# Sliding-window attention and a low-rank mixer on one core: load order, the order of chunk 0's second matmuls, one-slot values for two batches, and two copies of transposed Q/K

## The chip, the cores and the metric

The kernel runs on one core of one Trainium2 chip. A core has a matrix engine (TensorE, PE in the profile; PEld is its weight load), a vector engine (VectorE, DVE), a scalar engine (ScalarE, ACT), GpSimd (POOL), a queue engine (SyncE, SP) and 16 DMA engines. Each engine runs its own instructions in program order and waits for the others on semaphores. DMAs are issued here from POOL (loads that cast from float32 to bfloat16) and from SP (stores and transposes). The metric is the device time of one execution in microseconds (us), less is better.

## The reference

There are 8 batches of 576 tokens, 8 heads of 64 dimensions. Each query sees its own key and the 63 before it. The attention's output goes, laid out as (batch, token, 512), through a low-rank mixing over tokens and an MLP, both with a residual.

```python
mask = (rel >= 0) & (rel < 64)                      # rel = query position - key position
attn = softmax(where(mask, q @ k.T / 8, -1e9))
x = (attn @ v)                                      # as (batch, 576, 512)
u = x + ((x.transpose(0, 2, 1) @ U) @ V).transpose(0, 2, 1)   # U: 576x32, V: 32x576
out = u + maximum(u @ w_ch1, 0) @ w_ch2             # 512x2048, 2048x512
```

## The kernel before

**Chunks and slots.** The 4608 tokens of all batches are cut into 9 chunks of 512. For each chunk c the MLP is a list of 32 steps of four matmuls: 16 first matmuls `ch1(i)` (a `psA` tile, then a relu `c1_i` on DVE or ACT, as the lists `DVE_RELU` say) and 16 second ones `ch2(t, quarter)`, four token tiles t in four quarters of the inner dimension. After the last quarter DVE adds `u` into `osb`, and SP stores it. Each step is followed by a slot, a list of pieces of the next batch's attention (b = c + 1). The tables `PLACE`, `PLACE_1` (chunk 0, batch 1) and `PLACE_2` (chunk 1, batch 2) give each piece its slot. The program's order on every engine is written out by these tables; nothing is rescheduled. Slot 31 is the last one of a chunk that has a step ahead of it.

**Attention of one batch.** Q and K must stand transposed in `qf` and `kf`. For batches 0 and 1 the loads are grouped (`kg`, `qg`) and PE transposes them (pieces T). From batch 2 on they are loaded in five token tiles into `kn`, `qn`, and SP transposes them by DMA (pieces TX, ten a batch). There is one `kf` and one `qf` for all batches. Pieces S are the scores of head pairs with their exponent on ACT; SC8 is the same for the last 64 queries, the only one that reads token tile 4. M multiplies by the mask on DVE. PV multiplies by the values: for batches 0 to 2 one piece for each token tile (`PV(t)`), from batch 3 on all of them in one (`PVA`), which needs two `ps_big` buffers, one `ps_tp` and one `mm` buffer (`xe`). DVE divides by the sums and writes `xs`. U and V are the low-rank products (`pshh`, `psv`; DVE then adds into `un`). UT transposes `un` into `uTc`, which the next chunk's first matmuls read: on PE through the single `ps_tp` buffer with a copy on ACT for batches 1 and 2, and by SP's DMA from batch 3 on.

**Values.** The values stand in `vA`; `vB` holds the same rows moved by 64, copied from `vA` (`shift_v`): by POOL for batches 0 and 1, by DVE in slot 8 or 24 for the later ones.

**PSUM.** After the start the pool `mm` has three buffers, used in turn by `psA`, `psU`, `xe` and SC8's `high`. `ps_big` has two, `ps_tp` one.

**POOL's queue.** In this order: K and Q of batch 0, V of batch 0, w1 in halves, seven V copies, K and Q of batch 1, V of batch 1, w2 in four quarters, seven V copies, then for batches 2 to 7 K/Q and V. A DMA waits until the eighth before it has landed.

**SP's queue.** In program order: the stores of chunk c and the transposes of the slots. In chunk 0 the first store stands ahead of batch 2's transposes, which begin in slot 20; the others stand among and behind them.

Of the kernel before, what the change touches and what calls it, by code (L numbers as in the profile page):

```python
# [8 lines left out]
ACT = mybir.ActivationFunctionType  # L9
# [7 lines left out]
def kernel(  # L17
# [11 lines left out]
    nc = tc.nc  # L29
# [13 lines left out]
    NXB = 2  # L43
    NXU = 3
    GP = S // GR
# [13 lines left out]
    const = ctx.enter_context(tc.tile_pool(name="const", bufs=1))  # L59
    kg_pool = ctx.enter_context(tc.tile_pool(name="kg", bufs=4))  # L60
    uT_pool = ctx.enter_context(tc.tile_pool(name="uT", bufs=3))
# [28 lines left out]
    vB = [const.tile([P, NFULL, H, VW], BF16, name=f"vB{i}") for i in range(2)]  # L90
    kn = [const.tile([P, NT, H, D], BF16, name=f"kn{i}") for i in range(2)]
    qn = [const.tile([P, NT, H, D], BF16, name=f"qn{i}") for i in range(2)]

    kf = const.tile([P, NT * HP * P], BF16, name="kf")
    qf = const.tile([P, NT * HP * P], BF16, name="qf")
    kt, qt = ([f[:, j * S : (j + 1) * S] for j in range(HP)] for f in (kf, qf))
    kx, qx = (f.rearrange("p (t j w) -> p t j w", t=NT, j=HP) for f in (kf, qf))
    pts = const.tile([P, HP, 2, NB - 1, W], BF16, name="pts")
# [5 lines left out]
    def load_kq(b, split):  # L104
        grouped = b < NGR
        if grouped:
            kb = kg_pool.tile([GP, H, GR, D], BF16, name="kg")
            qb = kg_pool.tile([GP, H, GR, D], BF16, name="qg")
        else:
            kb, qb = kn[b % 2], qn[b % 2]  # L110
        loaded[b] = (kb, qb)
        if grouped:
            step = 4 if split else H
            for h0 in range(0, H, step):
                hs = slice(h0, h0 + step)
                for t, src in ((kb, k), (qb, q)):
                    nc.gpsimd.dma_start(  # L117
                        out=t[:, hs, :, :].rearrange("p h c d -> p h (c d)"),
                        in_=src[b, hs, :, :].rearrange("h (p c) d -> p h (c d)", c=GR),
                    )  # L120
                    yield
        else:
            for t in range(NT):
                rows = P if t < NFULL else W
                for dst, src in ((kb, k), (qb, q)):
                    nc.gpsimd.dma_start(  # L126
                        out=dst[0:rows, t, :, :],
                        in_=src[b, :, t * P : t * P + rows, :].rearrange("h p d -> p h d"),
                    )
                yield  # L130
# [15 lines left out]
    def shift_v(b, copy, tiles):  # L146
        va, vb = vA[b % 2], vB[b % 2]
        lo, hi = tiles.start, tiles.stop
        copy(out=vb[W:P, lo:hi, :, :], in_=va[W:P, lo:hi, :, :])
        last = min(hi, NFULL - 1)  # L150
        if lo < last:
            copy(out=vb[0:W, lo:last, :, :], in_=va[0:W, lo + 1 : last + 1, :, :])


# [38 lines left out]
    for i in range(2):  # L193
        nc.vector.memset(kn[i][W:P, NFULL, :, :], 0.0)
        nc.vector.memset(qn[i][W:P, NFULL, :, :], 0.0)

# [19 lines left out]
    for lo, hi in ((0, 1024), (1024, 2048)):  # L216
        nc.gpsimd.dma_start(out=w1b[:, :, lo:hi], in_=w1v[:, :, lo:hi])
    for t in range(NFULL):
        shift_v(0, nc.gpsimd.tensor_copy, range(t, t + 1))
    for _ in load_kq(1, False):  # L220
        pass
    load_v(1)
    w2v = moe_w_ch2.rearrange("(i p) m -> p i m", p=P)
    for i in range(0, NFC, 4):
        nc.gpsimd.dma_start(out=w2b[:, i : i + 4, :], in_=w2v[:, i : i + 4, :])
    for t in range(NFULL):
        shift_v(1, nc.gpsimd.tensor_copy, range(t, t + 1))

# [9 lines left out]
    def attention(b, spare=False):  # L238
# [5 lines left out]
        g0 = (b * S) // P  # L244
        pcs = {}

        grouped = b < NGR
# [28 lines left out]
        def TQ(j):  # L276
            def f():
                copy = nc.scalar.copy if spare and j == 3 else nc.vector.tensor_copy
                copy(out=place_of(qt, j), in_=tr(qb, j, b == 1))
            return f  # L280
# [80 lines left out]
        def SC8():  # L361
            if b >= NXU:

# [225 lines left out]
        def UT(t):  # L589
            def f():  # L590
                g = g0 + t
                dst = uT_of(g // TPC)[:, g % TPC, :, :]
                if b >= NXU:
                    nc.sync.dma_start_transpose(out=dst, in_=u_tiles[g][:])  # L594
                    return
# [13 lines left out]
        pcs["B"] = [SB(j) for j in range(HP + 1)]  # L609
        pcs["S"].insert(0 if b >= NXU else HP, SC8)  # L610
        if not spare:
            pcs["M"] = [MK(j) for j in range(HP)]
            pcs["M"].insert(0 if b >= NXU else HP, MK8)
        pcs["PV"] = [PVA] if b >= NXU else [PV(t) for t in range(NT)]
        pcs["U"] = [UM((t,)) for t in range(NT)] if spare else [UM(tuple(range(NT)))]
# [15 lines left out]

    DVE_RELU = {0: (8, 10, 11, 13, 15), 1: (2, 4, 6, 9, 10, 12, 13)}
    DVE_RELU_N = (0, 1, 2, 4, 5, 6, 8)

    def mlp(c):
        uTc = uT_of(c)
        c1 = [None] * NFC

        def ch1(i):
            def f():  # L640
                ps = psum["mm"].tile([P, CH], FP32, name="psA", tag="mm")
                for dc in range(NDC):
                    nc.tensor.matmul(  # L643
                        ps[:],
                        w1b[:, dc, i * P : (i + 1) * P],
                        uTc[:, :, dc, :],
                        start=(dc == 0),
                        stop=(dc == NDC - 1),
                    )
                c1[i] = c1_pool.tile([P, CH], BF16, name=f"c1_{i}")  # L650
                if i in DVE_RELU.get(c, DVE_RELU_N):
                    nc.vector.tensor_relu(out=c1[i][:], in_=ps[:])  # L652
                else:
                    nc.scalar.activation(out=c1[i][:], in_=ps[:], func=ACT.Relu)  # L654
            return f
# [23 lines left out]

        return [ch1(i) for i in range(NFC)] + [ch2(t, r) for t in range(TPC) for r in range(4)]  # L680

# [4 lines left out]
        "PV": [8],  # L686
        "TX": [6, 7, 8, 9, 10],
        "U": [14],
# [4 lines left out]
    PLACE_1 = {  # L693
        "T": [11, 11, 12, 12, 13, 13, 14, 14],
        "S": [12, 13, 14, 15, 15],
        "M": [13, 14, 15, 16, 16],
        "PV": [17, 17, 18, 19, 20],
        "U": [22],
        "V": [23, 24, 25],
        "UT": [25, 26, 27, 28, 29],  # L700
        "TX": [20, 22, 24, 26, 28],
    }
    PLACE_2 = {
        "S": [8, 8, 11, 11, 13],
        "M": [9, 10, 12, 13, 14],
        "PV": [16, 16, 18, 18, 20],
        "TX": [13, 14, 15, 16, 17],
        "U": [21],
        "V": [23, 24, 25],
        "UT": [25, 26, 27, 28, 29],  # L710
    }
# [4 lines left out]
    def turn_over(n, cols=CH):  # L716
# [16 lines left out]
    )  # L733
    pair = maskA[:, 0, 1:3, :].rearrange("p (o n) w -> p o (n w)", o=1)
    nc.vector.tensor_copy(
        out=maskA[:, 0, 3:7, :].rearrange("p (o n) w -> p o (n w)", o=2),
        in_=pair.to_broadcast([P, 2, 2 * W]),
    )
    nc.vector.tensor_copy(out=maskA[:, 0, 7, :], in_=maskA[:, 0, 1, :])
    nc.vector.tensor_scalar(  # L740
        out=maskB[:],
        in0=maskA[:, 0, :, :],
        scalar1=30000.0,
        scalar2=-30000.0,
        op0=ALU.mult,
        op1=ALU.add,
    )
    order = "K0 K1 B0 B1 Q0 Q1 S0 S1 K2 K3 B2 Q2 B3 Q3 S2 S3 B4 S4"
    for what in order.split():
        j = int(what[1])  # L750
        if what[0] in "SB":
            a[what[0]][j]()
        else:
            a["T"][2 * j + (what[0] == "Q")]()
        if what == "Q1":
            load_low_rank()
        turn_over({"B1": 1, "Q1": 1, "S1": 1, "Q3": 1}.get(what, 0))
    nc.vector.tensor_copy(out=maskA[:, 1, :, :], in_=maskA[:, 0, :, :])
    nc.scalar.copy(out=ub[0][:], in_=uf[0][:])
    nc.scalar.copy(out=vrep[:, W : W + S], in_=vf[:])  # L760
    for t in range(NT + 2):
# [7 lines left out]
    for f in [a["U"][NT - 1]] + a["X3"] + a["HT"]:  # L769
        f()  # L770
    first.close()
    psum["mm"] = ctx.enter_context(
        tc.tile_pool(name="ps_mm", bufs=3, space=bass.MemoryType.PSUM)
    )


    for c in range(NCH):
        slots = [[] for _ in range(NSLOT + 1)]

        def place(b, parts, where):  # L780
            if b not in att:
                att[b] = attention(b)
            for part in parts:
                for f, s in zip(att[b][part], where[part]):
                    slots[s].append(f)

        b = c + 1
        if b < B:
# [5 lines left out]
            if b + 2 < B:  # L794
                for _ in load_kq(b + 2, False):
                    pass
            where = {1: PLACE_1, 2: PLACE_2}.get(b, PLACE)
# [5 lines left out]
            for bs, slot in ((b, 8), (b + 1, 24)):  # L803
                if 1 < bs < B and (slot == 24) == (bs > 2):
                    slots[slot].append(
                        lambda bs=bs: shift_v(bs, nc.vector.tensor_copy, range(NFULL))
                    )
            place(b, ("S", "M", "PV"), where)
            if NXB <= b + 1 < B:
# [36 lines left out]
```

The softmax here doesn't subtract the row's maximum and nothing guards it: scores larger than these inputs give would overflow.

## Time and profile before

| | us |
|---|---|
| median of 7 runs | 321.74 (320.65 to 322.82) |
| the profiled execution | 320.83 |
| its span, first to last instruction | 319.1 |
| start to the first `psA` matmul | 23.41 |
| PE busy | 305.1 (96%) |
| DVE, ACT, POOL busy | 163.0, 101.8, 103.9 |

The span is shorter than the execution's time by 1.7 us, which lie outside of what the profile's instructions cover. A group's line in the profile reads: source line, engine, operation, output<-inputs, shape, count, then busy time and mean; in a timeline the bracket tells how long the engine was idle before and what released it. PE's busy time counts overlapping instructions once, so that the 379 ns of one 128x512 matmul is its passage through a pipeline: 36 of them in a row start 0.216 us apart. DMA shares over 1 say that packets of several queues lay in the same engine at once. Two group lines show what the two kinds of loads and stores look like:

```profile
vA<-in_v_dram POOLq DMA_DIRECT2D x32, 128.0 KB, 11.4
kf<-kn SPq DMA_TRANSPOSE x30, 7.9
```

The last number is the median time from issue to landing in us.

### The profile page before, as it was taken

How to read it: one execution, taken by the hardware profiler on the slowest of the kernel's cores; microseconds unless marked ns; L12 is line 12 of the kernel's file. 1: busy time of each engine (PE TensorE's matmuls, PEld its weight loads, DVE VectorE, ACT ScalarE, POOL GpSimd, SP SyncE). 2: the span in 40 equal slices, each digit the busy share in tenths (PEclk: the TensorE clock that was granted, in tenths of full speed). 3: DMA queues.
4: the chain of work that ended last, by engine and by line, in shares of the span. 5: the costliest groups of instructions: out<-in, count | busy, mean ns of one | idle time of the engine just before them, and what ended most of it. 6: DMA issues, size and time to landing. Idle time of an engine off the chain costs nothing.

```text
span 319.1 us, 6811 instructions
## 1 busy us (share of the span) xinstructions
PE 305.1 (96%) x2829; PEld 149.2 (47%) x2855; DVE 163.0 (51%) x293; ACT 101.8 (32%) x160; POOL 103.9 (33%) x134
## 2 busy tenths in 40 slices
PE   7779988999989999999999999999999999999995
PEld 6544543544445544454445444544454444444442
DVE  4464675447656755475547454756474443016011
ACT  3645550337124440345033502350245003201500
POOL 8692697444844744555543400000000000000000
PEclk9999999999999999999999999999999999999999
DMA  7999999999999999999999994444200520020011
GB/s 110 162 224 201 154 200 172 102 175 189 153 124 212 165 130 143 198 174 156 127 204 172 131 171 159 68 100 92 108 2 2 115 100 2 13 86 33 2 66 66
DMA packets 151871, 39.56 MB, mean 124 GB/s; under 512 B 140960, under 2 KB 146080, under 8 KB 151840
## 3 DMA queue, kind: packets, MB, share of 16 engines
q0 software_dynamic: 100096, 18.36, 82.8%
q1 hardware_dynamic: 51744, 20.77, 37.3%
q8 instruction: 22, 0.36, 0.5%
q14 instruction: 9, 0.07, 0.1%
HBM read 37.14 MB, written 9.44 MB: 146 GB/s over the span
## 4 chain that ended last, share of the span: by engine, by line
PE 66%; DMA 26%; POOL 3%; issue 2%; DVE 1%; SPq 1%; POOLq 0%; DVEq 0%
PE psA L643 31%; PE psU L665 29%; DMA vA<-in_v_dram 10%; DMA qg<-in_q_dram 5%; DMA kn<-in_k_dram 4%; DMA w2b<-in_moe_w_ch_dram 4%; DMA uTc<-un 3%; PE psv L566 2%; PE sc L326 2%; PE xw L388 2%; POOL vA L135 1%; POOL kg L117 1%; SPq L594 1%; PE pshh L487 1%; DVE osb L674 0%
## 5 line engine op out<-in xcount | busy, mean ns | idle before, releaser
L665 PE MATMUL psU<-w2b,c 128*128 128x512 bf16 x555 | 130.3, 379 | 3.4 <-DMA w2b<-in_moe_w_ch_dram 2.0
L643 PE MATMUL psA<-uTc,w1b 128*128 128x512 bf16 x576 | 131.0, 380 | 0.8 <-DVE uTc L553 0.4
L665 PEld LDWEIGHTS <-c 128*128 128x128 bf16 x576 | 55.3, 98 | 66.5 <-issue 2.8
L643 PEld LDWEIGHTS <-w1b 128*128 128x128 bf16 x576 | 54.0, 98 | 65.5 <-issue 1.3
L654 ACT ACTIVATE c<-psA 128x512 bf16<-128x512 f32 x83 | 49.6, 597 | 91.3 <-PE psA L643 91.3
L674 DVE TENSOR_TENSOR osb<-psU,un 128x512 f32<-128x512 f32 x36 | 24.9, 690 | 82.9 <-PE psU L665 82.7
L652 DVE TENSOR_SCALAR c<-psA 128x512 bf16<-128x512 f32 x61 | 42.0, 689 | 24.9 <-PE psA L643 24.9
L579 DVE TENSOR_TENSOR un<-psv,xs 128x512 bf16<-128x512 f32 (+1 forms) x40 | 25.4, 683 | 22.1 <-PE psv L566 22.0
L126 POOL DMA_DIRECT2D qn<-in_q_dram x30 | 25.5, 849 | 26.9 <-DMA vA<-in_v_dram 15.3
L135 POOL DMA_DIRECT2D vA<-in_v_dram x32 | 28.5, 898 | 17.7 <-PE psA L643 3.7
L346 ACT ACTIVATE pts<-sc 128x1024 bf16<-128x1024 f32 x32 | 31.4, 1030 | 2.5 <-PE sc L326 2.4
L126 POOL DMA_DIRECT2D kn<-in_k_dram x30 | 25.8, 861 | 11.5 <-DMA vA<-in_v_dram 7.3
L379 ACT ACTIVATE ptl<-low 128x256 bf16<-128x256 f32 x5 | 1.9, 383 | 65.1 <-PE high L326 65.1
L352 DVE TENSOR_TENSOR pts<-pts,maskA 128x1024 bf16<-128x1024 bf16 x28 | 19.1, 681 | 0.1
L326 PEld LDWEIGHTS <-kf 64*64 64x64 bf16 x704 | 10.0, 107 | 8.3 <-issue 7.7
L326 PE MATMUL sc<-qf,kf 64*64 64x128 bf16 (+1 forms) x624 | 12.2, 212 | 1.4 <-issue 0.8
L388 PEld LDWEIGHTS <-pts 128*64 128x64 bf16 x512 | 10.2, 110 | 6.2 <-issue 3.3
L566 PE MATMUL psv<-hh,vrep 128*128 128x512 bf16 x40 | 12.6, 379 | 0.0
L455 DVE TENSOR_TENSOR xs<-xw,rcw 128x896 bf16<-128x896 f32 x10 | 10.9, 1091 | 0.3
L411 DVE TENSOR_TENSOR xs<-xr,rcp 128x512 bf16<-128x512 f32 (+1 forms) x15 | 10.4, 690 | 0.5
L502 ACT CAST hh<-pshh 128x512 bf16<-128x512 f32 x7 | 4.1, 581 | 16.7 <-PE pshh L495 16.7
L601 ACT COPY uTc<-tpu 128x512 bf16<-128x512 bf16 x9 | 5.3, 585 | 12.3 <-PE tpu L598 12.3
(102 smaller groups left out, 160.1 us busy)
## 6 DMA issues: line engine op xcount, KB each, us to landing
out_dram<-osb SPq DMA_DIRECT2D x36, 256.0 KB, 3.3
vA<-in_v_dram POOLq DMA_DIRECT2D x32, 128.0 KB, 11.4
kn<-in_k_dram POOLq DMA_DIRECT2D x24, 128.0 KB, 12.4
qn<-in_q_dram POOLq DMA_DIRECT2D x24, 128.0 KB, 12.0
w1b<-in_moe_w_ch_dram POOLq DMA_DIRECT2D x2, 1024.0 KB, 15.9
w2b<-in_moe_w_ch_dram POOLq DMA_DIRECT2D x4, 512.0 KB, 12.7
kg<-in_k_dram POOLq DMA_DIRECT2D x2, 288.0 KB, 5.4
qg<-in_q_dram POOLq DMA_DIRECT2D x2, 288.0 KB, 6.2
```

What stands on the lines that cost most here:

```text
L126: nc.gpsimd.dma_start(out=dst[0:rows, t, :, :], in_=src[b, :, t * P : t * P + rows, :].rearrange("h p d -> p h d"),)
L135: nc.gpsimd.dma_start(out=va[:, t, :, 0:D], in_=v[b, :, t * P : (t + 1) * P, :].rearrange("h p d -> p h d"),)
L326: nc.tensor.matmul(sc[g][r0 : r0 + W, col * W : (col + n) * W], keys_of(j, u, rs), queries_of(j, blk, n, rs), start=not spare, stop=last o ...
L346: nc.scalar.activation(out=dst, in_=sc[:], func=ACT.Exp, scale=scale)
L352: nc.vector.tensor_tensor(out=dst, in0=dst, in1=maskA.rearrange("p g n w -> p g (n w)"), op=ALU.mult)
L566: nc.tensor.matmul(ps[0][:, n, :], vrep[:, off : off + P], hh["sb"][:], start=True, stop=True)
L579: nc.vector.tensor_tensor(out=u_tiles[g][rs, :], in0=ps[0][rs, n, :], in1=x[rs, t, :, :].rearrange("p h d -> p (h d)"), op=ALU.add,)
L643: nc.tensor.matmul(ps[:], w1b[:, dc, i * P : (i + 1) * P], uTc[:, :, dc, :], start=(dc == 0), stop=(dc == NDC - 1),)
L652: nc.vector.tensor_relu(out=c1[i][:], in_=ps[:])
L654: nc.scalar.activation(out=c1[i][:], in_=ps[:], func=ACT.Relu)
L665: nc.tensor.matmul(acc[t][:], c1[i][:, t * P : (t + 1) * P], w2b[:, i, :], start=(i == 0), stop=(i == NFC - 1),)
L674: nc.vector.tensor_tensor(out=osb[:], in0=acc[t][:], in1=u_tiles[g][:], op=ALU.add)
```

## The change

- **Loads.** Batch 1's V is loaded between the two halves of w2, not ahead of it. K and Q of batches 0 and 1 no longer have tiles of their own (`kg`, `qg`), but use the memory of `kn`, `qn` (`kr`, `qr`); K and Q of batch 3 are therefore requested in slot 14 of chunk 0, after batch 1's transposes. POOL's order of loads is otherwise unchanged.
- **V copies.** Of batch 0's seven, five stay on POOL and two go to ACT. Batch 1's seven leave POOL: four on ACT, three on DVE, in slots 16 and 17 of chunk 0 (`SV`).
- **Chunk 0.** The first two steps are interleaved. The second matmuls run in pairs of token tiles: quarter 0 of tile 0, of tile 1, quarter 1 of tile 0, and so on. Batch 1's T and S come one slot sooner. PVA takes the place of five PV pieces, in slot 19. U is in slot 25 (from 22), V in 26 to 28 (from 23 to 25), UT in 29, 30, 31, 31, and the fifth in slot 2 of chunk 1 (102). Batch 2's TX are in 24 to 28 (from 20 to 28).
- **Chunk 1.** Batch 2 has SC8 first, in slot 8 with the first two head pairs, as later batches have it; PVA in slot 16; UT in 26 to 29 (from 25 to 28); batch 3's TX in 9 to 13 (from 13 to 17).
- **Transposed Q/K.** Two each of `kf`, `qf`, by the batch's parity; from chunk 2 on TX is in slots 0 to 4 (from 6 to 10).
- **Start and relu.** The mask for batch 0 is built from three blocks, the rest by ACT and later DVE; one idle matmul is added; the fourth Q copy of batch 0 moves from ACT to DVE; other steps have their relu on DVE in chunks 0, 1 and 2.

```diff
-    kn = [const.tile([P, NT, H, D], BF16, name=f"kn{i}") for i in range(2)]
-    qn = [const.tile([P, NT, H, D], BF16, name=f"qn{i}") for i in range(2)]
-    kf = const.tile([P, NT * HP * P], BF16, name="kf")
-    qf = const.tile([P, NT * HP * P], BF16, name="qf")
+    kr = [const.tile([P, H * GR * D], BF16, name=f"kr{i}") for i in range(2)]
+    qr = [const.tile([P, H * GR * D], BF16, name=f"qr{i}") for i in range(2)]
+    kn, qn = (
+        [r[:, 0 : NT * DM].rearrange("p (t h d) -> p t h d", t=NT, h=H) for r in rs] for rs in (kr, qr)
+    )
+    kfs = [const.tile([P, NT * HP * P], BF16, name=f"kf{i}") for i in range(2)]
+    qfs = [const.tile([P, NT * HP * P], BF16, name=f"qf{i}") for i in range(2)]
...
+    def shift_high(b, copy, t):
+        copy(out=vB[b % 2][W:P, t, :, :], in_=vA[b % 2][W:P, t, :, :])
+
+    def shift_low(b, copy, t):
+        copy(out=vB[b % 2][0:W, t, :, :], in_=vA[b % 2][0:W, t + 1, :, :])
...
-    for t in range(NFULL):
-        shift_v(0, nc.gpsimd.tensor_copy, range(t, t + 1))
+    for t in range(2):
+        shift_high(0, nc.gpsimd.tensor_copy, t)
+        shift_low(0, nc.gpsimd.tensor_copy, t)
+    shift_low(0, nc.gpsimd.tensor_copy, 2)
...
-    load_v(1)
     for i in range(0, NFC, 4):
+        if i == NFC // 2:
+            load_v(1)
         nc.gpsimd.dma_start(out=w2b[:, i : i + 4, :], in_=w2v[:, i : i + 4, :])
-    for t in range(NFULL):
-        shift_v(1, nc.gpsimd.tensor_copy, range(t, t + 1))
...
-        pcs["S"].insert(0 if b >= NXU else HP, SC8)
+        pcs["S"].insert(0 if b >= NGR else HP, SC8)
-        pcs["PV"] = [PVA] if b >= NXU else [PV(t) for t in range(NT)]
+        pcs["PV"] = [PVA] if not spare else [PV(t) for t in range(NT)]
...
-    DVE_RELU = {0: (8, 10, 11, 13, 15), 1: (2, 4, 6, 9, 10, 12, 13)}
+    DVE_RELU = {0: (7, 9, 11, 15), 1: (2, 4, 6, 8, 10, 12, 15), 2: (1, 3, 6, 7, 9, 10)}
...
-        return [ch1(i) for i in range(NFC)] + [ch2(t, r) for t in range(TPC) for r in range(4)]
+        ups = [ch1(i) for i in range(NFC)]
+        if c == 0:
+            ups[0:2] = [ch1(0, 1), lambda: None]
+            return ups + [ch2(t, r) for u in (0, 2) for r in range(4) for t in (u, u + 1)]
+        return ups + [ch2(t, r) for t in range(TPC) for r in range(4)]
...
     PLACE = {
-        "TX": [6, 7, 8, 9, 10],
+        "TX": [0, 1, 2, 3, 4],
     PLACE_1 = {
-        "T": [11, 11, 12, 12, 13, 13, 14, 14],
-        "S": [12, 13, 14, 15, 15],
-        "M": [13, 14, 15, 16, 16],
-        "PV": [17, 17, 18, 19, 20],
+        "T": [10, 10, 11, 11, 12, 12, 13, 13],
+        "S": [11, 12, 13, 14, 15],
+        "M": [12, 13, 14, 15, 16],
+        "SV": [16, 16, 17, 17],
+        "PV": [19],
+        "U": [25],
+        "V": [26, 27, 28],
+        "UT": [29, 30, 31, 31, 102],
+        "TX": [24, 25, 26, 27, 28],
-        "U": [22],
-        "V": [23, 24, 25],
-        "UT": [25, 26, 27, 28, 29],
-        "TX": [20, 22, 24, 26, 28],
     PLACE_2 = {
-        "S": [8, 8, 11, 11, 13],
-        "M": [9, 10, 12, 13, 14],
-        "PV": [16, 16, 18, 18, 20],
-        "TX": [13, 14, 15, 16, 17],
-        "U": [21],
-        "UT": [25, 26, 27, 28, 29],
+        "S": [8, 8, 8, 11, 11],
+        "M": [8, 9, 10, 12, 13],
+        "PV": [16],
+        "TX": [9, 10, 11, 12, 13],
+        "U": [22],
+        "UT": [26, 27, 28, 29],
...
-        turn_over({"B1": 1, "Q1": 1, "S1": 1, "Q3": 1}.get(what, 0))
+        turn_over({"B1": 1, "Q1": 1, "S1": 1, "B2": 1, "Q3": 1}.get(what, 0))
+    for t in range(2, NFULL):
+        shift_high(0, nc.scalar.copy, t)
...
+                def land(t):
+                    def f():
+                        shift_high(1, nc.scalar.copy, t)
+                        if t > 0:
+                            shift_low(1, nc.vector.tensor_copy, t - 1)
+                    return f
```

## The prediction

> **What bounds the kernel now.** First the chain of waits and the clock row of the page, then the stretches between the first `psA` matmuls of two chunks (stretch, length, busy time of PE, PEld, DVE, ACT, POOL with counts, PE clock, DMA share, GB/s):
>
> ```profile
> PE 66%; DMA 26%; POOL 3%; issue 2%; DVE 1%; SPq 1%; POOLq 0%; DVEq 0%
> PEclk9999999999999999999999999999999999999999
> ...
> 23.41:63.98 40.57, 38.17 (x419) 19.26 (x424) 22.53 (x38) 16.95 (x28) 24.48 (x32) 1.00 2.07 167
> 63.98:98.95 34.97, 33.77 (x316) 16.27 (x318) 20.26 (x35) 12.56 (x19) 18.13 (x22) 1.00 1.86 163
> 98.95:131.58 32.63, 32.15 (x301) 15.13 (x301) 19.20 (x33) 10.17 (x16) 17.53 (x21) 1.00 2.00 159
> 131.58:163.84 32.26, 32.16 (x300) 15.31 (x303) 18.29 (x32) 10.17 (x16) 16.73 (x20) 1.00 1.80 163
> 163.84:195.94 32.10, 31.99 (x301) 15.23 (x301) 18.61 (x32) 10.17 (x16) 8.19 (x10) 1.00 1.73 178
> ```
>
> From chunk 3 on TensorE has no idle time: 32.10 us a chunk, whatever the other engines do. DMA carries weight in the chain (26%), all of it before 132 us. So there is something to win only in chunk 0 (40.57), chunk 1 (34.97) and, by 0.5, in chunk 2 (32.63). Next the timeline of PE in chunks 0 and 1:
>
> ```profile
> 46.56 1.02 PE L665 MATMUL psU<-w2b,c 128*128 128x512 bf16 x4 [0.85 <-DMA w2b<-in_moe_w_ch_dram]
> 49.10 1.02 PE L665 MATMUL psU<-w2b,c 128*128 128x512 bf16 x3 [1.14 <-DMA w2b<-in_moe_w_ch_dram]
> ...
> 71.84 0.71 PE L326 MATMUL sc<-qf,kf 64*64 64x128 bf16 x36
> ...
> 95.04 0.40 PE L598 MATMUL tpu<-ident,un 128*128 128x128 bf16 x4 [0.94 <-DVE un L579]
> ```
>
> Two waits for w2b, 2.0 us, and one of 0.94 for `un`, behind the V shift that waits for batch 3's V (landed 92.6). The scores of batch 2 at 71.84 just miss a wait: the last transposed Q of token tile 3 lands at 72.0 by the trace's landing times, tile 4 at 75.6; tile 4 is read only by SC8, in slot 13. Last, SP's queue, which issues these transposes:
>
> ```profile
> 50.88 0.37 SPq L677 DMA_DIRECT2D out_dram<-osb  x1
> 51.44 1.31 SPq L285 DMA_TRANSPOSE kf<-kn  x1
> 52.85 1.23 SPq L285 DMA_TRANSPOSE qf<-qn  x1
> ...
> 68.39 1.30 SPq L285 DMA_TRANSPOSE qf<-qn  x1
> ```
>
> Ten transposes of batch 2, first issue 51.44, last landing 75.6: 24.2 us. For the later batches the same span is 22.9 (75.7 to 98.7), 23.7 (103.9 to 127.6), 23.7 (136.5 to 160.2) and 21.9 (168.6 to 190.5). Only batch 7, when no loads run any more, takes 15.0 (200.7 to 215.7).
>
> **The change, part by part.**
>
> *Start-up.* Half the mask and one Q copy change engine, one idle matmul (0.22 us) is added, and two of POOL's seven V copies (0.62 each) go to ACT. The first chunk still waits for the first half of w1b, which lands at 23.2 and is issued before all of that: 0. If that cover were gone, the matmul would cost its 0.22. POOL then issues K and Q of batch 1 some 0.6 us sooner, but they queue behind w1b's second half (landed 28.2), so their landings at 31.2 and 34.8 stay.
>
> *w2b and batch 1's V.* The bytes are the same and the DMAs have no gap there, so the last half of w2b lands at 49.1 as before, V about 5 us later (about 44.5 for 39.6). Chunk 0's second matmuls now use w2b's third quarter after four steps, not two. Start of slot 16: 42.9 before, plus 0.5, since transposes moved to slot 10 reach Q of batch 1 at 34.3, and it lands at 34.8. So slot 16 at about 43.0 to 43.4, and four steps of 0.863 later slot 19 ends at 46.5. PVA takes 1.29 (141.02 to 142.31 in the chain). Third quarter at 47.8 (landed 46.5), fourth at 49.5 (landed 49.1): both waits gone, −2.0. One PVA for five PV tiles of 0.5 each: −1.2 of PE in chunk 0, the same in chunk 1.
>
> *V copies.* Four ACT copies of 64x520: no row on ACT. Nearest are POOL's 0.62 for the same shape and ACT's 0.64 for 128x576; bounds 0.3 to 0.65, I take 0.62 by the same shape. They start behind S8's exp at about 43.7, end at about 46.2, just before PVA. Cost 0; at the upper end 0.2. POOL's other seven copies hid under the loads anyway: 0.
>
> *Two new waits in chunk 0.* (a) Pairs keep two `psU` and PVA's `xe` in the three `mm` buffers, so the third token tile's `psU` in slot 24 waits for the first `osb`. That add stands on DVE behind all of PVA's normalisation:
>
> ```profile
> 108.38 0.35 PE xw L388 x14
> ...
> 109.58 0.18 DVE L444 RECIPROCAL rce<-xe 128x4 f32<-128x4 f32 x1 [0.48 <-PE xe L388]
> 112.90 0.86 DVE L467 TENSOR_TENSOR xs<-one,rco 64x256 bf16<-64x256 f32 x2
> ```
>
> So it ends 5.4 us after PVA's start; with `osb` (0.69) 6.1. PE would be there after 1.29 + 4 × 0.863 = 4.74: +1.35. (b) `UT` of tiles 2 and 3 both come after the last step, on a single `tp` buffer; each takes 0.42 to its ACT copy, 0.58 for the copy, some 0.06 to the next. Chunk 1's first matmul reads the result: 2.1 us less 0.44 of work, +1.65. Chunk 0 is then 32.1 + 1.1 (batch 0's V) + 2.6 (transposes) + 0.9 (UT) + 0.5 + 1.35 + 1.65 = 40.2: chunk 1 starts at 63.5, 0.5 sooner than now. Most of the win is given back.
>
> *Chunk 1, the decisive step.* Batch 2's SC8 now comes first, in slot 8, and reads token tile 4. PE reaches slot 8 at 63.5 + 9 × 0.863 + 0.22 = 71.5. In SP's compiled order two output stores now stand ahead of the ten transposes, and both wait for `osb`. PVA's start at 46.5 plus 6.1 is 52.6, the second add 53.2, two stores of about 0.6: first transpose at 53.9 instead of 51.44. Its K and Q have landed since 50.8; they only queue behind the stores. Ten transposes: bounds 15.0 (no load) and 24.2, I take 23, the middle of the rows under load, since the loads of batches 2 and 3 run then. Two stores fewer stand among them, which would save some 1.5 of the 24.2. Tile 4 lands at 76.9. PE waits 5.4 us in slot 8, with everything behind it. From there 32.1 + 0.9 of UT + 0.2 − 9 × 0.863 − 0.2 = 25.2: chunk 2 starts at 102.1 for 98.95, **+3.15**. The V shift of slot 24 comes at about 94.5; V of batch 3, with two or three transposes more ahead of it at some 0.9 each, lands at about 95, and the UT that needs it stands one slot later than before: no further wait.
>
> *Double Q/K, early transposes (chunks 2 on).* The Trainium skill ("Trainium Kernel Development and Optimization", Best Practices) says to double-buffer so that DMA overlaps compute; by that rule these chunks should gain. The rows show 32.10 us with no idle PE, so the sum by the row is 0. SP gets to chunk 2's `uTc` transposes sooner, so its end (0.37 <- DMA uTc) may vanish: −0.4. Chunk 0's interleaved first two steps, the new relu lists: 0, PE waits for neither.
>
> *A clock that falls.* No PE wait in this trace is over 1.4 us and the clock row is full throughout, so it shows nothing of a 5 us wait. The skill ("TensorE: Matmul & The Clock Gate", Part 1) states that one idle window of some 3.4 us, running freely, halves the clock until a busy one has passed. By the row 0; by the rule an estimate of half of 3.4, +1.7, if a whole window falls into the 5.4 us, about even odds. I take 0, since a shorter wait escapes it, and keep +1.7 as the upper end.
>
> **Sum.** +3.15 − 0.4 = +2.75. The profiled execution took 320.83 (span 319.1); so 323.6 there, and on the median of 321.74, 0.9 above it, 324.5.
>
> **Rivals.**
> - *As forecast, and the clock falls* (+1.7): 326.2. For it the length of the wait, against it that it must hold a whole window. 0.30.
> - *Faster:* the ten transposes land by 71.5, 17.6 us after their first issue, because no store interrupts them. Then chunk 2 starts at 71.5 + 25.2 = 96.7, −2.25 − 0.4: 319.1. It decides at 18.5 us or less for the ten; four of four rows under load say 22 and more, only the one without load 15. 0.13.
> - *Nothing:* the transposes land at about 73 and V of batch 3, later for them, holds the UT of slot 28: about 98 + 3.0 for the rest, so 98 to 101 as chunk 2's start, −1.3 to +1.6: 321.7. 0.09.
> - The forecast itself, 323 to 325.8 (22 to 24.2 us for the ten): 0.48.
>
> **Numbers.** What this kernel's measurement can tell from no change is about 0.3%, 1 us. Faster 0.13, same 0.09, slower 0.78. The range leaves out the faster case's lower part and the longest clock drop: 320.8 to 327.0; the likeliest case's own range is 323 to 325.8.
>
> **What would show it.** Right: a PE wait of 4 to 7 us before `low` in chunk 1, ended by a DMA `kf` or `qf`; first batch 2 transpose on SP at about 54, after two stores; waits of about 1.4 at slot 24 and 1.6 at chunk 1's first `psA`; no w2b wait; clock below 1.00 in that stretch only if the rule bites. Wrong: transposes at 51 or landing before 72, or chunk 1's `low` without a wait. A step short of 32.1 us in chunks 3 to 6 would overturn the reading that PE bounds them.

## The result, and the profile after

The changed kernel takes 329.01 us (median of 12 runs, 327.94 to 331.87) beside 321.67 for the kernel before (31 runs on the same chip): a ratio of 1.0235, 95% interval 1.021 to 1.026. The forecast was 324.5, its range ended at 327.0: the direction held, the size did not. The profiled execution took 329.05, its span is 327.3. Ratios and their intervals, here and below, leave out runs over 1.5% above the fastest of their kernel (one of e3's, two of e13's, at most two of the kernel before in each comparison).

Two lines of the page, the chain of waits and the granted PE clock in 40 slices:

```profile
PE 90%; DMA 4%; DVE 3%; ACT 1%; issue 1%; SPq 0%; ACTq 0%; POOLq 0%
PEclk9959999996999999999999999999999999999999
```

PE now carries 90% of the chain for 66%, DMA 4% for 26%. Read alone, that looks like a better kernel. But the clock row has two dents, a 5 and a 6, where before there were only nines. The stretches between the first `psA` matmuls of two chunks (the same columns as before) say where the time went:

```profile
25.96:65.62 39.66, 37.71 (x415) 18.79 (x419) 23.61 (x43) 18.74 (x32) 24.03 (x29) 1.00 1.85 175
65.62:105.97 40.35, 34.55 (x318) 17.04 (x321) 19.74 (x33) 13.21 (x21) 20.97 (x25) 0.92 1.84 162
105.97:139.81 33.84, 32.30 (x300) 15.19 (x301) 18.28 (x31) 10.45 (x17) 16.90 (x21) 1.00 1.97 155
139.81:171.90 32.09, 31.98 (x300) 15.20 (x301) 18.60 (x32) 10.17 (x16) 12.58 (x15) 1.00 1.93 165
```

Chunk 0 is 0.9 shorter (39.66 for 40.57), chunk 1 is 5.4 longer (40.35 for 34.97, at a mean clock of 0.92), chunk 2 is 1.2 longer (33.84 for 32.63). From chunk 3 on nothing has changed. And the first `psA` comes 2.55 later, at 25.96. The timeline of PE shows each wait (the bracket is the idle time ahead of it and what ended it):

```profile
55.45 1.02 PE L676 MATMUL psU<-w2b,c 128*128 128x512 bf16 x4 [0.44 <-DVE osb L685]
...
64.56 0.38 PE L607 MATMUL tpu<-ident,un 128*128 128x128 bf16 x4 [0.67 <-ACT uTc L610]
65.62 2.75 PE L653 MATMUL psA<-uTc,w1b 128*128 128x512 bf16 x12 [0.67 <-ACT uTc L610]
79.31 0.23 PE L335 MATMUL low<-qf,kf 64*64 64x64 bf16 x1 [5.54 <-DMA qf<-qr]
120.13 1.02 PE L653 MATMUL psA<-uTc,w1b 128*128 128x512 bf16 x4 [0.74 <-ACT c L665]
121.84 1.89 PE L653 MATMUL psA<-uTc,w1b 128*128 128x512 bf16 x8 [0.69 <-ACT c L665]
```

No wait for w2b is left. In its place stand small waits in chunk 0, one of 5.54 in slot 8 of chunk 1, and two in chunk 2 that the forecast did not have. SP's queue shows why the transposed Q is late: two stores, which wait for `osb`, are ahead of the first transpose.

```profile
55.42 0.95 SPq L688 DMA_DIRECT2D out_dram<-osb  x2
56.56 1.78 SPq L294 DMA_TRANSPOSE kf<-kr  x1
...
71.98 1.39 SPq L294 DMA_TRANSPOSE qf<-qr  x1
```

The ten take from 56.56 to the last landing at 79.18 (the last one lands 7.2 after its issue), 22.6 us.

### The profile page after: what moved, and what is told of

It reads as the page before. It is cut to its first block, busy times and chain, and to the rows that moved or that the text cites. A ratio compares the mean times of both kernels' runs of the same rounds, so it can differ in the third digit from the quotient of the medians.

```text
span 327.3 us, 6836 instructions
## 1 busy us (share of the span) xinstructions
PE 307.7 (94%) x2831; PEld 150.1 (46%) x2856; DVE 163.2 (50%) x294; ACT 105.4 (32%) x169; POOL 97.1 (30%) x125
## 4 chain that ended last, share of the span: by engine, by line
PE 90%; DMA 4%; DVE 3%; ACT 1%; issue 1%; SPq 0%; ACTq 0%; POOLq 0%
PE psA L653 39%; PE psU L676 37%; PE sc L335 3%; PE psv L575 3%; DMA qf<-qr 2%; PE xw L397 2%; DMA kr<-in_k_dram 1%; PE tpg L272 1%; PE pshh L496 1%; PE xr L397 1%; PE tpu L607 1%; DVE qf L288 1%; DVE xs L464 1%; PE sc L325 1%; PE psh L496 1%
## 5 line engine op out<-in xcount | busy, mean ns | idle before, releaser
L653 PE MATMUL psA<-uTc,w1b 128*128 128x512 bf16 x576 | 132.5, 382 | 2.5 <-ACT c L665 1.4
L665 ACT ACTIVATE c<-psA 128x512 bf16<-128x512 f32 x85 | 50.6, 598 | 93.5 <-PE psA L653 93.4
L663 DVE TENSOR_SCALAR c<-psA 128x512 bf16<-128x512 f32 x59 | 40.6, 689 | 27.0 <-PE psA L653 27.0
L126 POOL DMA_DIRECT2D kr<-in_k_dram x30 | 25.7, 858 | 15.4 <-DMA vA<-in_v_dram 6.4
L126 POOL DMA_DIRECT2D qr<-in_q_dram x30 | 25.7, 855 | 10.8 <-DMA vA<-in_v_dram 4.8
L464 DVE TENSOR_TENSOR xs<-xw,rcw 128x896 bf16<-128x896 f32 x14 | 15.3, 1091 | 0.5
L397 PE MATMUL xw<-vA,pts 128*64 128x65 bf16 x217 | 8.4, 195 | 0.0
```

The lines of the kernel that those rows point to most:

```text
L126: nc.gpsimd.dma_start(out=dst[0:rows, t, :, :], in_=src[b, :, t * P : t * P + rows, :].rearrange("h p d -> p h d"),)
L397: nc.tensor.matmul(dst, pts[:, h // 2, h % 2, blk, :] if blk < NB - 1 else ptl[:, h // 2, h % 2, :], rhs, start=True, stop=True,)
L653: nc.tensor.matmul(ps[i][:], w1b[:, dc, i * P : (i + 1) * P], uTc[:, :, dc, :], start=(dc == 0), stop=(dc == NDC - 1),)
L663: nc.vector.tensor_relu(out=c1[i][:], in_=ps[i][:])
L665: nc.scalar.activation(out=c1[i][:], in_=ps[i][:], func=ACT.Relu)
```

## The experiments

The theory after the first look: slot 8 waits for transposes that stand behind the stores; that wait then lowers the clock, which costs again; chunk 2 is long because of the new relu list. All edits are on the changed kernel (329.0) unless something else is said; a ratio is always to the kernel before, in runs on the same chip. The runs were on five chips, on which the medians of the kernel before lie between 321.5 and 322.3, so that a difference between the medians of two runs is uncertain by up to 0.8.

**e1: batch 2's transposes ahead of the stores.**

```diff
-        "TX": [24, 25, 26, 27, 28],
+        "TX": [18, 18, 19, 19, 20],
```

> The changed kernel (329.0) with batch 2's ten transposes issued from slots 18 to 20 of chunk 0, so that on SP they stand ahead of the two output stores that wait for osb. Theory (the stores set the first transpose's issue, and the wait in slot 8 is paid once as a wait and once more by the clock): first transpose at about 52 to 53, last landing about 75 to 76, the wait in slot 8 down from 5.5 to about 2, no clock drop in chunk 1: 3.5 to 5 us less, 324 to 325.5. Rival (the loads' traffic sets when the ten are through, whenever they begin): landing stays at about 79, the wait at about 5, time 328 to 329.

Measured: 323.92, ratio 1.0060 (1.0031 to 1.0088), 5.1 us less by the medians, 5.6 by the ratios. SP's queue in e1, its PE timeline, and DVE in slot 24:

```profile
50.14 1.30 SPq L294 DMA_TRANSPOSE kf<-kr  x1
```

```profile
73.45 0.19 PE L335 MATMUL low<-qf,kf 64*64 64x64 bf16 x1 [1.16 <-DMA qf<-qr]
```

```profile
95.50 0.70 DVE L149 COPY vB<-vA 64x2080 bf16<-64x2080 bf16 x1 [3.73 <-DMA vA<-in_v_dram]
```

The first transpose starts at 50.14, as soon as K has landed (49.98), and the ten are through at 73.3: 23.2 us, much as with the later start. So it is the start that sets their end, and the rival is out. The wait in slot 8 is 1.16 and the clock stays at 1.00 in this profile. A next wait shows up: DVE holds the copies of batch 3's V in slot 24 until V lands, batch 2's last three `un` are behind them, and PE waits 2.00 for it.

**e2: SC8 last again for batch 2.**

```diff
-        pcs["S"].insert(0 if b >= NGR else HP, SC8)
+        pcs["S"].insert(0 if b >= NXT else HP, SC8)
...
-        "S": [8, 8, 8, 11, 11],
+        "S": [8, 8, 11, 11, 13],
```

(M likewise.)

> The changed kernel with batch 2's SC8 and MK8 behind the other scores, in slot 13, as the kernel before has them; the transposes stay where they are. Theory: slot 8 then needs only token tile 3 (landed at 76.8 in the changed kernel's profile), its wait falls from 5.5 to about 3, and slot 13 waits for nothing; if the clock's drop needs a wait of more than 3.4, it goes too: 2.5 without, 4 with: 325 to 326.5. Rival (the order of SC8 doesn't matter, since the transposes of tile 3 come just before those of tile 4): under 1 us gained.

Measured: 324.18, ratio 1.0073 (1.0048 to 1.0098), 4.8 less, a little more than expected. Slot 8 waits 2.60, now for token tile 3; slot 13 does not wait. I had expected no lower clock for a wait shorter than the prediction's window of some 3.4. It came in the profiled execution, for half as long. The stretches ahead of it and in it:

```profile
72.34:75.76 3.42, 1.41 (x29) 0.87 (x29) 1.56 (x3) 1.10 (x2) 2.06 (x3) 1.00 1.71 156
75.76:79.18 3.42, 3.42 (x15) 0.99 (x16) 1.94 (x3) 1.33 (x2) 1.56 (x2) 0.50 1.50 245
```

It does not come every time: six of e2's twenty executions have a mean clock of 0.997 or more, with a median of 322.9; the other fourteen have 0.995 or less, with 324.7.

**e7: the kernel before with SC8 first, this one part alone.**

```diff
-            if b >= NXU:
+            if b >= NGR:
                 low = ps_tp.tile([P, CH], FP32, name="low", tag="tp")
...
-        pcs["S"].insert(0 if b >= NXU else HP, SC8)
+        pcs["S"].insert(0 if b >= NGR else HP, SC8)
...
-        "S": [8, 8, 11, 11, 13],
+        "S": [8, 8, 8, 11, 11],
```

(M likewise.)

> The kernel before with one part of the change alone: batch 2's SC8 and MK8 first, in slot 8, in their two single banks. Theory (tile 4, which lands at 75.6 there, is wanted 3.8 too early): a wait of 3 to 4 before low in slot 8, DMA qf at its end, 3 to 4 more than the kernel before if the clock holds (325 to 326), up to 1.5 more if it falls. Rival (the change's other parts, not this one, are what makes the scores wait): within 1 us of the kernel before.

Measured: 325.54, ratio 1.0107 (1.0082 to 1.0133), 3.8 more than before. In its PE timeline:

```profile
75.30 0.23 PE L326 MATMUL low<-qf,kf 64*64 64x64 bf16 x1 [3.55 <-DMA qf<-qn]
```

The tile wanted too early is enough for a wait of 3.55, with a clock of 0.50 from 73.92 to 80.75 beside it. That the rest of the changed kernel's wait, 2.0, comes from the later start of the transposes (56.56 for 51.27 here) is by subtraction; e1 shows that the start matters.

**e4: the wait filled with idle matmuls.**

```diff
                 banks = [low[:], high[:]]
+                if b == NGR:
+                    for _ in range(20):
+                        nc.tensor.matmul(low[:], idle[:, 0:P], idle[:], start=True, stop=True)
```

> The changed kernel with 20 matmuls of 128x512 on constant data (4.3 us at full clock) into low ahead of batch 2's SC8, inside the wait of 5.5 in slot 8; they compute nothing that is kept. Theory (the wait's idle time halves the clock for 6.8 us behind it, which costs some 1.5): clock 1.00 through chunk 1, chunk 1's stretch behind slot 8 back from 26.7 to about 25.2, 327.3 to 327.6. Rival (what is lost behind slot 8 is late work on other engines, not the clock): 329 or, if the fill runs over the wait, more.

Measured: 326.16, ratio 1.0134 (1.0068 to 1.0200; four runs), a larger gain than expected. The fill (19 of its twenty matmuls are in the trace) and what is left of the wait, in e4's PE timeline, and the stretch from slot 8 to chunk 2:

```profile
71.93 4.48 PE L378 MATMUL low<-idle 128*128 128x512 bf16 x19
78.51 0.19 PE L335 MATMUL low<-qf,kf 64*64 64x64 bf16 x1 [2.10 <-DMA qf<-qr]
```

```profile
78.51:103.64 25.13, 24.86 (x279) 12.67 (x282) 15.38 (x27) 9.53 (x15) 12.43 (x15) 1.00 1.82 162
```

The changed kernel, first profile: the stretch ahead of the drop, the drop, and the same stretch from slot 8 to chunk 2:

```profile
72.39:75.81 3.42, 1.38 (x7) 0.42 (x5) 2.32 (x4) 0.60 (x1) 1.44 (x3) 1.00 1.72 156
75.81:82.64 6.83, 3.33 (x58) 1.86 (x59) 1.13 (x3) 2.68 (x5) 3.93 (x5) 0.50 1.59 199
79.31:105.97 26.66, 26.39 (x278) 13.37 (x282) 15.72 (x27) 9.64 (x15) 13.92 (x17) 0.94 1.88 160
```

The scores still wait for the same DMA, 4.48 of fill and then 2.10, but behind them the work takes 25.13 at full clock, where the changed kernel took 26.66 at 0.94. Matmuls that compute nothing made the kernel faster. What was lost behind slot 8 was the clock.

**e3: chunk 2 without a relu list of its own.** DVE's timeline in chunk 2 of the changed kernel has two relus (`c<-psA`) behind the whole normalisation of PVA:

```profile
116.60 0.18 DVE L453 RECIPROCAL rce<-xe 128x4 f32<-128x4 f32 x1 [1.33 <-PE xe L397]
...
119.92 0.86 DVE L476 TENSOR_TENSOR xs<-one,rco 64x256 bf16<-64x256 f32 x2
120.81 1.29 DVE L663 TENSOR_SCALAR c<-psA 128x512 bf16<-128x512 f32 x2
```

```diff
-    DVE_RELU = {0: (7, 9, 11, 15), 1: (2, 4, 6, 8, 10, 12, 15), 2: (1, 3, 6, 7, 9, 10)}
+    DVE_RELU = {0: (7, 9, 11, 15), 1: (2, 4, 6, 8, 10, 12, 15)}
```

> The changed kernel without chunk 2's own list of relus on DVE; chunk 2 falls back on the list of the later chunks (0, 1, 2, 4, 5, 6, 8). Theory: relus 9 and 10 stood on DVE behind PVA's normalisation and held mm buffers; without them PE's waits of 0.74 and 0.69 in chunk 2 go and it takes 32.6 or less for 33.84: 327.6 to 328. Rival (those waits come from uTc or a load, not from DVE): 329.0.

Measured: 327.18 for four runs that scatter from 324.78 to 330.61, ratio 1.0133 (1.0043 to 1.0223). By the time alone it can't be told from the changed kernel (1.021 to 1.026). Chunk 2's stretch in its profile, which is of the slowest of the four:

```profile
109.25:141.34 32.09, 31.98 (x301) 15.16 (x302) 18.67 (x32) 10.17 (x16) 17.56 (x21) 1.00 2.13 155
```

1.75 less than 33.84, no wait; e5 below has the same 32.09. The list in the later chunks ends with step 8, ahead of PVA's slot. The waits of 0.74 and 0.69 in the changed kernel are shown under ACT: two of the three `mm` buffers wait for their relus on DVE, so PE has one buffer left and can go on only when ACT has done the relu of the step before (at 120.08 and 121.79 by its timeline).

**e5: the three edits together.**

> The three edits of e1, e2 and e3 together on the changed kernel: batch 2's transposes ahead of the stores, its SC8 and MK8 last, chunk 2's relus as the later chunks have them. Theory (the three losses are separate and add): no wait at slot 8 (tile 3 lands at about 72), chunk 2 at 32.1 for 33.84; what stays is the wait for batch 3's V at the transposes of un (2.0 in e1): chunk starts at 23.6, 63.6, 99, 131, so 320 to 321, 1.3 to 2.3 below the kernel before. Rival (each of the edits only moves the same wait on, to V of batch 3): chunk 1 as long as in e1, 36.6 or more, 322 or above.

Measured: 320.83, ratio 0.9984 (0.9960 to 1.0009): no slower than before, no difference that can be told. Chunks 0 to 2 take 40.28, 34.94 and 32.09. Slot 8 does not wait; V of batch 3 costs 1.33.

**e6: also the V copies of batch 3 in slot 31, and batch 1's UT one slot earlier.**

```diff
-                    slots[slot].append(
+                    slots[31 if bs == 3 else slot].append(
...
-        "UT": [29, 30, 31, 31, 102],
+        "UT": [27, 28, 29, 30, 102],
```

> e5 with two edits more: the copies of batch 3's V moved from slot 24 to slot 31 of chunk 1, behind the adds of batch 2's un on DVE, and batch 1's transposes of un one slot earlier each (27 to 30), so that none is issued behind the last second matmul. Theory: the wait for V (2.0) goes and so do the waits of 0.67 at the end of chunk 0: 2 to 2.7 less than e5, 318 to 319. Rival (DVE is late anyway, so un and V's copies are late in the next place): under 1 us less than e5.

Measured: 318.29, ratio 0.9891 (0.9853 to 0.9929): faster than the kernel before. Chunk 0 takes 38.32, chunk 1 33.44. Chunk 2 takes 33.68: batch 3's Q is now 1.38 late in its slot 0.

**e8: e6 without pairs in chunk 0.**

```diff
-            return ups + [ch2(t, r) for u in (0, 2) for r in range(4) for t in (u, u + 1)]
+            return ups + [ch2(t, r) for t in range(TPC) for r in range(4)]
```

> e6 with chunk 0's second matmuls in the order of the kernel before, one token tile after the other, no pairs; PVA and the V between w2b's halves stay. w2b's third quarter is then wanted in the third step and the fourth in the fourth. Theory (pairs are what gives w2b's last quarters the time to land): waits for w2b of 1.5 to 2.5 at the third and fourth step, and 1.2 to 2 more than e6. Rival (w2b lands early enough, or PVA between the steps covers it): as e6, within 0.5.

Measured: 318.80, ratio 0.9919 (0.9887 to 0.9950). The intervals of e6 and e8 overlap, so the medians do not decide. e8's PE timeline does:

```profile
46.89 1.02 PE L676 MATMUL psU<-w2b,c 128*128 128x512 bf16 x4 [0.99 <-DMA w2b<-in_moe_w_ch_dram]
49.42 1.47 PE L676 MATMUL psU<-w2b,c 128*128 128x512 bf16 x4 [1.51 <-DMA w2b<-in_moe_w_ch_dram]
```

The waits for w2b are back, 2.50 in all, and chunk 0 takes 41.93 (with 3.41 us at half clock behind the waits), 3.6 more than in e6. Of that 1.6 is given back in chunk 2, at 32.10: it starts at 99.37 for 95.46, and batch 3's Q is no longer late. The profile is of the slowest of the five executions; the other four, at clocks of 0.998 or more, took 318.15 to 319.05, so the lower clock does not belong to every execution of e8.

**e9: e6 with batch 3's scores from slot 2 on.**

```diff
+    PLACE_3 = {**PLACE, "S": [2, 2, 2, 4, 4], "M": [2, 3, 4, 5, 6]}
```

> e6 with batch 3's scores two slots later in chunk 2 (from slot 2 on instead of slot 0). In e6 batch 3's last transposed Q is late by 1.38 in slot 0 of chunk 2. Theory (the only idle time left there is that landing): chunk 2 at 32.1 for 33.7, 1.4 to 1.6 less than e6: span about 315.1, 316.7 to 317. Rival (PVA in slot 8 then waits for its masks, or the DMAs come later again): as e6, 318.3.

Measured: 317.57, ratio 0.9889 (0.9852 to 0.9926), four runs; with e10 below the best version found, 1.1% below the kernel before, though not told from e6 by these intervals. Its stretches by chunk:

```profile
23.47:61.76 38.29, 37.58 (x415) 18.83 (x419) 23.16 (x42) 18.74 (x32) 19.11 (x23) 1.00 1.90 167
61.76:95.21 33.45, 33.19 (x320) 16.32 (x322) 18.61 (x32) 13.10 (x21) 16.87 (x20) 1.00 1.91 162
95.21:127.93 32.72, 32.49 (x301) 15.28 (x301) 19.93 (x35) 10.07 (x16) 15.59 (x19) 1.00 1.83 160
```

PE's idle time is 0.7, 0.3 and 0.2. Chunk 2 lost 1.0, not the 1.4 to 1.6 expected.

**e12: e9 with values by token tile for batches 1 and 2.**

```diff
-        pcs["PV"] = [PVA] if not spare else [PV(t) for t in range(NT)]
+        pcs["PV"] = [PVA] if b >= NXT else [PV(t) for t in range(NT)]
```

(Slots 18, 18, 19, 19, 20 and 16, 16, 17, 17, 18.)

> e9 with batch 1's and 2's values by token tile, five of 0.5 on PE instead of one PVA of 1.29, batch 1's in slots 18 to 20. Theory (PVA saves 1.2 of PE in each of chunks 0 and 1): chunk 0 longer by 0.8 to 1.2, since the wait of 0.44 for osb goes and a wait for w2b may go with it, chunk 1 by 1.2: 2 to 2.4 more than e9. Rival (PVA's long normalisation on DVE takes back what it saves): within 0.8 of e9.

Measured: 318.85, ratio 0.9928 (0.9898 to 0.9957), 1.3 more than e9, somewhat over half of what was expected. Chunk 0 is 38.93 for 38.29, chunk 1 34.48 for 33.45: PVA saves 0.64 and 1.03. In chunk 0 part of the saving goes into the wait of 0.44 for `osb`, which the tiles do not have.

**e11 and e13: one transposed Q/K.**

```diff
-        kf, qf = kfs[odd], qfs[odd]
+        kf, qf = kfs[0], qfs[0]
```

> e9 with one transposed Q/K in place of two. A batch's transposes then wait for the scores of the batch before. Theory: batch 2's (slots 18 to 20 of chunk 0, its predecessor's scores end in slot 15) lose nothing; batch 3's, in slots 9 to 13 of chunk 1, wait for scores until slot 13, land up to 4 later and bring a wait of 1 to 3 into chunk 2; from chunk 3 on the stretches stay at 32.09: 1 to 3 more than e9. Rival (a second Q/K brings nothing anywhere, as the prediction's 0 has it): within 0.5 of e9.

Measured: 379.35, far outside of both expectations. The edit did not test what it was meant to: in e9's order transposes stand ahead of some scores of the batch before. With one Q/K those scores read the next batch's Q and K and wait for them (waits of 8.71, 3.26 and 7.19 in chunk 1). So e13 puts the transposes behind the scores, where the kernel before has them:

```diff
     PLACE = {
-        "TX": [0, 1, 2, 3, 4],
+        "TX": [6, 7, 8, 9, 10],
     PLACE_2 = {
-        "TX": [9, 10, 11, 12, 13],
+        "TX": [13, 14, 15, 16, 17],
```

> e9 with one transposed Q/K and every batch's transposes behind all scores of its predecessor, as the kernel before places them (slots 13 to 17 of chunk 1, 6 to 10 of later chunks). In e11 they stood ahead of scores in slots 3 and 11, so that those scores read the next batch's Q and K and waited for them; its time measures that order. Theory (the second Q/K is worth only the earlier landing of batch 3's transposes, which slot 2 of chunk 2 needs): batch 3's land about 4 later than in e9, a wait of 1 to 4 in chunk 2, 0 in the later chunks: 318.5 to 321.5. Rival (the second pair is worth nothing here): within 0.7 of e9, 317.0 to 318.3.

Measured: 321.98, ratio 0.9987 (0.9961 to 1.0013), 4.4 more than e9 by the medians, 3.2 by the ratios; the forecast of the time missed by 0.5, and its place was wrong. Nothing waits for batch 3's scores. Instead chunk 3's first `psA` waits 2.91 for `uTc`, in e13's PE timeline:

```profile
131.63 0.82 PE L653 MATMUL psA<-uTc,w1b 128*128 128x512 bf16 x3 [2.91 <-DMA uTc<-un]
```

The reason is in SP's queue: SP reaches the `uTc` transposes at 120.34 in e13 and at 115.14 in e9, because Q and K's stand before them. Behind it the clock falls for 3.41, and chunk 3 takes 33.84. Of the twenty executions seven have a mean clock of 0.997 or more, with a median of 320.2; the other thirteen have 322.6. So the second Q/K, with the earlier slots that it permits, is worth about 3 to 4 us in e9's arrangement, a part of it through the clock.

**e10, e15 and e14: the start-up.** In the changed kernel's profile the start-up has a lower clock of its own:

```profile
14.37:17.79 3.42, 1.99 (x68) 1.46 (x65) 0.72 (x2) 3.08 (x6) 1.50 (x4) 1.00 1.30 206
17.79:24.61 6.82, 6.35 (x64) 3.43 (x66) 3.66 (x9) 1.89 (x5) 5.44 (x7) 0.50 1.22 218
```

Whether the new order of the start-up brings that on was open. e10 is e9 with the start-up of the kernel before, e15 the changed kernel with it, e14 the changed kernel unedited once more. The edit of both puts back the lines of the mask, of the idle matmul after B2, of the Q copy on ACT and of the seven V copies on POOL.

> e9 with the start-up of the kernel before: mask copies and batch 0's last Q copy on DVE and ACT as there, no idle matmul after B2, all of batch 0's V copies on POOL. Theory (the start-up's new order costs nothing, the lower clock at 17.8 in the changed kernel's profile comes by chance, in the kernel before too): first psA at 23.4 to 24.0 and the time of e9 within 0.5. Rival (the new order leaves PE idle longer and so brings the lower clock on): e10 faster than e9 by 1 or more, and its executions at a clock of 0.99 or more throughout.

> The changed kernel with the start-up of the kernel before (masks, last Q copy, no idle matmul after B2, V copies on POOL). Theory (start-up is 0): within 0.7 of the changed kernel. Rival (the new start-up order brings the lower clock on and costs the part of the miss that chunks 1 and 2 leave over): 1.5 or more less than the changed kernel, 327.5 or below.

> The changed kernel once more, unedited, for a second profile and more executions beside the kernel before. Theory (the start-up's lower clock is chance; when it is absent the slot 8 wait is longer, since the DMAs land at about the same time): 328.5 to 329.5; if its profile has no lower clock at 17.8, first psA at 23.4 to 24, slot 8 waits 6 to 7, chunk 2 starts at 104.5 to 105.5, span 326 to 326.6. Rival (the lower clock at start-up belongs to the changed kernel): first psA at about 26 again.

Measured: e10 317.57, ratio 0.9877 (0.9846 to 0.9908), as e9. e15 328.74, ratio 1.0200 (1.0159 to 1.0241), and e14 328.20, ratio 1.0202 (1.0161 to 1.0242): the same. No cost of the start-up's order can be seen. In e14's profile the first `psA` is at 23.97, without a lower clock at the start; of thirteen profiles with the new start-up only two, the first one and e3's, have it. Single runs of the kernel before go down to mean clocks of 0.989 to 0.984 as well; one stretch of 6.83 us at half clock makes 0.989 of its span.

In chunk 1, though, e14's clock falls again. Three stretches of it, the first one ahead of the drop, the second the drop, the third from slot 8 to chunk 2:

```profile
71.88:75.30 3.42, 0.15 (x1) 0.00 (x0) 1.95 (x3) 0.00 (x0) 1.77 (x3) 1.00 1.75 153
75.30:82.13 6.83, 4.66 (x61) 2.37 (x62) 1.12 (x2) 3.09 (x5) 3.26 (x4) 0.50 1.55 199
77.47:104.78 27.31, 27.31 (x281) 13.56 (x282) 15.67 (x27) 9.64 (x15) 14.77 (x18) 0.91 1.87 158
```

27.31 for e4's 25.13: here the clock costs 2.2, in the first profile it cost 1.5. The drops are equally long, but in e14 4.66 us of it lie behind the wait, which ends at 77.47, in the first profile 3.33; half of these, an estimate of the cost, is 2.3 and 1.7. Two things in e14's expectation failed. It had a wait of 6 to 7 in slot 8, since I thought that the late start of the first profile hid part of it; it was 5.44 (e15: 7.48, e3: 7.46, both with slot 8 as in the changed kernel). The wait varies by 2 us between executions. And its median, 328.2, is a little under the range of 328.5 to 329.5.

## Why the prediction was wrong

Against e14, whose start has no lower clock, the forecast's chain can be set beside the measured one. First the forecast, then e14, then the first profile:

| | forecast | e14 | first profile |
|---|---|---|---|
| first `psA` | 23.4 | 23.97 | 25.96 |
| chunk 0 | 40.1 | 39.91 | 39.66 |
| chunk 1 up to slot 8 | 8.0 | 8.15 | 8.15 |
| wait in slot 8 | 5.4 | 5.44 | 5.54 |
| slot 8 to chunk 2 | 25.2 | 27.31 | 26.66 |
| chunk 2 | 32.2 | 33.85 | 33.84 |
| chunk 3 to the end | 187.6 | 187.6 | 187.5 |

- **The decisive step was right, in kind and size.** SC8 first, transposes behind two stores, tile 4 too late: wait 5.4, measured 5.54 and 5.44, ended by `qf`. The first transpose was forecast at 53.9; it came at 54.81 in e14 with a start 0.6 later. The ten were put at 23; they took 22.6 in the first profile, 22.5 in e14, 24.5 in e15 and 23.5 in e4. The rival "faster", with 17.6 for them, is out. That the wait agrees to 0.1 is partly luck: where the ten took 24.5, in e15, it was 7.48.
- **The clock behind it failed.** The sum took 0 and kept +1.7 for the range's upper end, by the argument that a shorter wait escapes and that a whole idle window must fall into the wait ("TensorE: Matmul & The Clock Gate", Part 1, in the Trainium skill). Measured: 1.5 in the first profile and 2.2 in e14, and none of the 17 runs of the unedited kernel has a mean clock over 0.990. The row of the trace could not show it, since no wait in it was long enough; the rule named the mechanism and about the right price. The odds that I gave it were too low for this wait. And where the page asks for an idle window, the 3.42 ahead of a drop need not be idle: 1.38 of PE work in it (72.39 to 75.81 in the first profile) and 1.41 (e2) did not prevent the drop.
- **Chunk 2 failed: −0.4 forecast, +1.2 measured.** "The new relu lists: 0, PE waits for neither" was the step. It looked at DVE's load, not at its order. Relus 9 and 10 stand behind 4.2 us of normalisation and hold two of the three `mm` buffers. The row that I had quoted for PVA's normalisation in batch 3 was the one to lay beside the list. Without the list chunk 2 has 32.09 (e3, e5): the −0.4 is there as −0.5, and the list's +1.75 covers it.
- **Chunk 0's sum held, its terms less so.** Both waits for w2b are gone, as forecast (and back in e8). The wait for `osb` was put at 1.35, at the third token tile's `psU`. It measured 0.44 and stands one step later: PE issues five steps of second matmuls between PVA (its end is at 50.51 in the first profile) and the wait, not four. `xe`'s buffer, read by DVE by 51.1, was free for the third tile, and only the fourth tile's `psU` had to wait; 1.35 less one step of 0.863 is 0.49. The two waits around UT were put at 1.65 and measured 1.34. The saving of PVA was put at 1.2 and is 0.64 and 1.03 in chunks 0 and 1 of e12. The errors partly cancel.
- **Start-up: 0 was right**, as far as e10 and e15 can tell. Of the 2.55 in the first profile, 2.0 are not there in e14, whose start has the full clock; that the clock made them is argued, not shown. The start varies for other reasons too: in e15 the first `psA` is at 25.14 at full clock.
- **Double Q/K: 0 by the row, a gain by the skill's best practice of double buffering.** In the changed kernel no gain from it can be seen, and no run took it out there. In e9, where the other waits are gone, it is worth 3 to 4 us (e13), and the rule was right.

The miss, 4.3 at chunk 3's start in e14 (138.63 for 134.3), is 0.6 of start, −0.2 of chunk 0, 2.3 of chunk 1, of which the clock is 2.1, and 1.6 of chunk 2. The rival "as forecast, and the clock falls" (326.2) was nearer than the forecast; with chunk 2's 1.6 added it would have been 327.8. So two terms that the sum put at 0 failed: the clock behind the wait and the order of chunk 2's relus on DVE. What stays open: why the clock falls at start-up in some runs and not in others, and why it spares six of e2's executions.

## What to carry to other kernels

A wait on PE, in a kernel that keeps it busy otherwise, can cost twice: once as a wait and once more for the clock behind it (1.5 and 2.2 here). In the profiles of this case the clock fell behind every unfilled wait of 2.60 to 8.71 us in chunks 1 to 3, and in e8 behind 0.99 and 1.51 close together; behind 1.16 and 2.00 in e1 it did not. It is a risk and not a certainty, as e2's executions show, and it goes if idle matmuls fill the wait (e4). Before moving a transfer's consumer forward, follow the transfer back through the queue that issues it: what counts is the instruction ahead of it that waits for something else, here two stores. When a change is slower, its parts may still be good: the same diff with six of its settings (slots and lists) changed, e9, was 1.1% faster than the kernel before.

## What was not expected of the hardware

- The lower clock came in stretches of 6.83 or 3.41 us (in e11 of 23.89 too), always 0.50, and followed stretches of 3.42 in which PE was busy for 0.15 (e14), 1.38 and 1.99 (the first profile) and 1.41 (e2): partly idle was enough in these executions.
- Ten transposes took 22.5 to 24.6 us under load whether they began at 50.1 or at 56.6. Against e14 a start 4.7 earlier (e1) brought a landing 4.0 earlier.
